# Down projections of token-tile pairs by Strassen's product in a sparse-attention and feed-forward kernel

## The chip, the core and the metric

The kernel runs on one core of a Trainium2 chip. The metric is the device time of one execution in microseconds. Five engines work side by side, each through its own in-order queue: PE (TensorE, matrix products; PEld is its weight loads), DVE (VectorE), ACT (ScalarE), POOL (GpSimd) and SP (SyncE, here a queue for transfers only). POOL's queue also issues transfers.

## The reference, cut to what matters

```python
# attention: q, k, v are [4, 8, 768, 64]; chunks of 32 keys, six chunks kept for each query
k_min, k_max = k_chunks.min(3), k_chunks.max(3)
ub = sum(max(q * k_min, q * k_max))            # a bound for each query and chunk
top_chunks = argsort(where(causal, ub, -1e9))[..., -6:]
attn = softmax(where(selected & causal, q @ k.T / 8, -1e9))
x = (attn @ v)                                 # as 3072 tokens of 512
# feed-forward: w_in is [512, 2048], w_out is [2048, 512]
h = maximum(x @ w_in, 0)
out = (h * h) @ w_out
```

The change touches the last line alone. The result is float32; inside, the kernel works in bf16 with float32 sums.

## The kernel before, in words

There are four sequences of 768 tokens, six tiles of 128 tokens each. The first tile of each sequence needs no choice of chunks (six chunks would not be exceeded); the four first tiles form a feed-forward block of their own, which runs early. Each sequence then has a block of its five other tiles. So `ffn` (L1143) is called five times.

In a block, `turn` brings a tile of x into the layout with features on partitions: through PE for the block of first tiles and for sequence 0, by a transposing transfer on SP's queue for the last three sequences. `up` (L1176) computes one of 16 slices of 128 hidden features for a group of columns (256 for the first two tiles of a sequence, 384 for the other three): four matmuls, a relu out of PSUM on ACT or DVE (L1193, L1195), and the square on DVE (L1204), which lands in a buffer of the tag `h2`. `down` (L1207) computes one token tile of the output: 16 matmuls of 128x512 that accumulate in one PSUM bank (L1217), with the squared slice as the stationary operand and a 128-row slice of `w_out` as the moving one. Then ACT or DVE copies the bank to an `ob` buffer (L387, L389), and a transfer writes it out on SP's queue, or on POOL's for sequences 1 and 2. The last tile of the kernel is done in two column groups, 384 and 128.

The attention around it: scores (L1026; for the last sequence L1083), exponentials on ACT (L1050, L1121), causal masks on POOL or DVE (L1006, L1003), products with v (L1038, L1116), normalisation on DVE (L731, L733). For the last sequence the choice of chunks goes out to a table in device memory (L967) and comes back as a mask for each head pair, by four transfers of 336 KB each on SP's queue (L974); POOL then puts the causal part into it (L1006), and DVE applies it to the exponentials (L1130).

Nothing is scheduled on the chip. Every step is recorded with `plan.op`, and the long string `SEQUENCE` lists the numbers of all steps in the order in which they are taken up, with a letter where the engine could be chosen (`A`, `D`, `G` for ACT, DVE, POOL). `Plan.order` (L220) walks through that list, gives each step a start by a table of costs, and the steps are issued sorted by these starts. So the order of each engine's queue is fixed by the list and these costs, and any change to the steps comes with a new list. Buffers have tags with a fixed number of slots, and a step that needs a slot waits until its last user is through.

```python
plan = Plan({"tp": 1, "ps": 3, "av": 2, "ff": 2, "e": 8, "h2": NFI + 6, "ht": 3,
             "ob": 3, "kq": 4, "nt": 6, "set": 3, "seen": 3,
```

`tp`, `ps`, `av` and `ff` are PSUM tags, eight banks in all. `nt` holds rows of q and k on their way to a transposing transfer.

Of the kernel before, what the change touches and what calls it, by code (L numbers as in the profile page):

```python
# [46 lines left out]
4 0 23 1 131 2 18 6 20 8 62D 7 10A 19 150 5A 22 12A 134 136 9A 135D 21 11D 13A 24 14D  # L47
3A 25 132 133D 27 61D 17D 137 16 148 26 138 146 142 147D 31 149D 143 139 174 144 29
151 145 176 140 152 141 32 177D 156 153 188 175A 154 28 157 155 178 15A 158 179 159 33
162 180 190 163D 191A 30 189D 164 184 36 192 195 193D 34 160 196A 198 161D 201 46 197  # L50
199A 194 165 202A 200 185 35 170 181 186 203 166 187 37 182 171 183 172 167 173 40 286
206 168 280 169 207A 287 41 204 290D 205A 39 288 282A 211 289D 208 45 212D 281A 213
214 209D 284 215A 217 60 226 218A 283 51 223 210 285 42 227A 219 291 224A 343 292 220
44 216 345A 293 43 229 294 344A 225 295 221A 347 296 230A 52 235 298A 346 297A 54 232
300A 228 299A 236D 38 309 317 222 310 349 237 301 48 233A 238 350 302 351 47 313 352D
318 241 348 314 353D 50 239A 305 234 322 311G 354 306 240 303G 323 355 250 67 307D 356
242A 315D 326 55 357 251A 304 308 330 324D 358 327 312 316 319 49 252 334 325 243 359
335 244 53 363D 331 362D 361D 412 332G 245A 385 336G 413 338 386 247 328G 360D 56 339
231 415D 372 248A 59 368 253 414 369 320 416D 69 373 376 249 364 406 321 374G 365 380
370G 409 256 254A 366G 65 410 367 371 375 377 389 68 262 381 408D 390 411 329 246 401  # L60
397 407D 391G 333 417 378G 398 337 255 340 469 387G 341 418 393 399G 471A 257 66 419
342 402 379 382 64 420 263 394 421 395D 388 383 422 472 392 71 396 423A 400 403 258
424D 384 435 404 427 426D 264 425D 428 473 436 448 439 449 57 470D 431 259 440 405
429G 432 474 460 437D 441D 475 260A 72 443 476 430 461 265 261 477 433G 444 70 478D
452 480 453 434 268 73 481 479A 483 462D 456 58 482 464 457 269 484 78 465 458D 438
266A 485 442 731 104 486D 267 270 487D 732A 488D 75 489D 506 450D 490 734 507 498 454G
445 271 79 499 735 491 451 98 455 494 500D 459 733D 463 495 523 492G 466 446 511 74
524 467 274 447 512 468 81 272A 737 736 525D 515 739 519 496G 502 741D 520 493 77 497
275 738 503 105 740D 513G 516 742 85 504D 527 743 501 505 528 508 521D 794 517G 509
744 83 514 518 796A 522 526 510 529 276 117 530 99 745 795A 531 277 76 746 797 80 747  # L70
534 278A 63G 749D 535A 532 748D 750D 102 533A 584 760 751D 585A 764 798 539 765 768
542 540A 799 769 800 543D 578 86 761 802 536 90 579A 544 801 752 537A 572 541 82 753
766G 580 756 538 575 573A 803D 805 804D 576A 557 108 84 757 577 545 806 558A 857 574
754G 546A 807 548 762G 858A 89 777 549D 566 808 859A 560 550 547 781 94 809 773 561A
755 860 567A 551 778 758G 103 581 774 562 779G 759 568 763 582D 782 767 785 87 775D
810 559 552A 569 279 583 812A 553 91 554 783G 811A 570D 770 861 586 555A 776 813A 815
100 563 273 771 587A 556 863 862 814D 564A 780 784 772 588 866A 789 571 638 565 589A
865 786 95 864 590 790 867D 787G 868 816 591D 106 668 819 869 669A 788 88 827 817G 870
791 593 871 670A 592 818 639 872 109 828 594D 96 820 823 671 873 596 821G 875A 101
829G 672 824 836 640 874A 825G 595 837 597D 831 674 92 792 832 598 822 605 793 678A  # L80
107 826 830 606D 840 876A 878 676 833 599 126 879 834 673 835 877A 641 607 112 677A
600D 97 882 841 1112D 886 880G 608 838D 642A 601 675 883 839 128 894 609D 602 887 1054
116 611 603A 93 1053 895 890 842G 679 124 612A 614 604 891 613 881 884G 617 1237 615A
122 127 1113A 844 620 610 888G 1236 618A 118 885 843 643 621A 899 632 619 845 892G
1055 680 623 616 633A 113 622 900 903 681 848 624A 629 119 1238 682 904 1429 907 630A
626 114 634 1114 849 852 1119A 644 846G 110 1056 683 627A 1115 645 1181A 905G 850G
1057 684 853 120 847 1240 635 685D 1174A 631 115 911 625 1060 1173A 1120D 646 123 1061
901G 1430 636A 647 1239 908 1063 637 125 688A 909G 889 1062 1243 686A 650 1244 687A
1064 912 1118 893 1065 689 1246 648A 697 651 1117 698 1245 1180A 628 851 699G 693 1247
896 854 1116 690 701 1248 855 652 856 694 691G 1175 702 705 695G 692 129 111 714 706  # L90
696 897 1121 703D 898 722 715 726 1122 700 704 121 707 716G 1123 727 902 710 906 1124
910 711 718 653 1052D 723 130 712G 1051D 719 1059D 915 656 654A 1242D 720G 649 1125
1069A 1068D 657 1234A 913D 1250D 724D 1095 916 708 1091 1066D 658 1241A 1067D 709 1126
1092 1496 1103 1249D 914 713 1251A 717 1252D 721 725 1058D 917 1096 728 1099 729 659
1104 918 1235D 730 1100 1070 919 660A 1107 1101G 662 1097D 921 1427 1071 1093G 1105G
1108 1074 1072G 1426 663 1075 920 1129A 1176 1076G 1086 1078 1127A 1082 1073 1077 972
1083 1177 664 1492 1079 1084G 665 1087 1080G 1128D 970 1428 1130A 1493 1139 666A 1131
1081 1085 1088 971 1132 1494 1431 1143 1140 1432 1094 1133G 1135 922 1433 1136 655 925
1434 923A 661 1147 1435 926A 1098 1089 928 1436 1148 1152 927 929A 1437 931 924 1153
1090 1102 1156 1141D 932A 934 930 1495 1144 937 1154D 667 933 935A 1160 1145G 938A  # L100
1106 936 940 1137G 1448 1161 943 941A 1109 1164 939 944A 1438 946 942 1110 949 1111
947A 945 1497 1178 950A 952 1498 1157 961 948 953A 1500 1158G 1134 1168 962A 1162G 954
955 1165 963 1138 1499 964 956A 1166G 1142 957 967 965A 1501 1440 951 1146 1149 1449
968A 958 1442 1155 1441 976 959A 969 1169 966 1439 960 979 1502 977A 1159 1451 973
980A 1450 978 1150 982 1452 974A 981 1179 1163 985 1470 983A 988 986A 984 975 1453
989A 991 1454 1455 994 992A 990 1167 1151 1000 995A 987 1182 996 1001A 1006 1183 993
1003 1184 1007A 1444 1170 1185 1009 1004A 1446 1002 1456 1253 1010A 1008 1012 1443
1186 1005 1015 1187 1013A 1011 1254 1265 1016D 997 1447 1457 1021 1471 1022 1017 998D
1458 1023 1190A 999 1459 1189A 1018 1266 1024 1019D 1472 1188D 1027 1191D 1025D 1503
1200 1208 1473 1028 1020 1209 1171 1014 1201 1460 1255D 1204 1172 1196 1029 1202D 1197  # L110
1205 1198G 1213 1192 1030 1206G 1193 1214 1194G 1217 1031D 1256 1278 1215G 1218 1195
1199 1203 1032 1221 1279 1462 1207 1210 1229 1222 1461 1211 1225 1219G 1212 1033 1230
1464 1223G 1267D 1226 1280G 1463 1216 1026 1257 1274 1227D 1474 1220 1224 1275 1228
1231 1269 1258 1232 1034 1233 1270 1259G 1445 1286 1282 1287 1261 1276G 1035 1262 1283
1290 1263D 1288D 1260 1264 1268 1284D 1291 1271 1277 1281 1272 1285 1289 1273 1292
1514 1293 1294 1039 1524 1295 1521 1525 1040 1518 1522 1515 1296 1041 1516 1527 1519
1347 1036 1537 1528 1469 1520 1526 1346 1037D 1531 1475 1042 1534 1538 1038 1476 1045
1345 1043A 1477 1467 1478 1044 1517 1523 1532 1297 1535 1046 1468 1298A 1529 1479 1300
1480 1540 1301A 1299 1481 1530 1302 1541 1533 1465 1303 1546 1047 1466 1304D 1554 1547
1309 1551 1555 1539 1548 1310D 1048 1552 1482 1549 1542 1306 1049A 1550 1557 1305  # L120
1307D 1553 1558 1312 1311 1308 1360 1567 1313D 1564 1559 1315 1568 1361A 1536 1543
1565 1560 1316A 1321 1561 1314 1544 1484 1318 1362 1322A 1545 1485 1570 1319A 1317
1562 1504 1556 1571 1342 1323 1486 1320 1324 1577 1343D 1483 1566 1574 1572 1563 1569
1327 1325D 1582 1573 1326 1357 1328A 1344 1575 1330 1578 1358A 1587 1329 1331A 1583
1336 1332 1597 1359 1351 1594 1337D 1591 1576 1333 1352D 1584 1579 1334A 1353 1339
1507 1585 1354 1586 1340A 1508 1338 1588 1335 1363 1505 1355A 1506 1600 1364A 1356
# [21 lines left out]
class Transfers:  # L148


    RATE = 1 / 0.00083
    SHARED = ((6.2, 0.90), (9.0, 0.95), (1e9, 1.0))
    ISSUED = {True: 0.7, False: 1.3}
    LANDED = {True: 1.3, False: 1.9}

# [156 lines left out]
def kernel(  # L312
# [943 lines left out]
    for t in range(B):  # L1256
        down(t)
# [65 lines left out]
```

## Time and profile before

| | us |
|---|---|
| runs shown: lowest, median, highest | 259.96, 260.93, 261.01 |
| profiled execution, its time | 260.51 |
| its span in the trace | 258.8 |
| granted TensorE clock, mean | 0.998 |

The 1.7 us between the profiled execution's time and its span lie outside the trace's span. A page of the profile gives the busy time of each engine, then the span in 40 slices (a digit is tenths of a slice), transfers, the chain of work that ended last, and the costliest groups of instructions. A group's row reads: line, engine, operation, output from inputs, sizes, count, busy time, mean nanoseconds of one, and the idle time just before them with what ended it. A matmul's own duration includes its way through the array, so the durations of neighbours overlap; the chain of waits shows what each adds.

### The profile page before, as it was taken

To read this page: it belongs to the slowest core of one execution; us is meant where nothing else is said; L and a number is where in the kernel's file an instruction comes from. 1 tells how busy PE (TensorE), PEld (TensorE's weight loads), DVE (VectorE), ACT (ScalarE), POOL (GpSimd) and SP (SyncE) were. 2 spreads that over 40 slices of the span, in tenths; PEclk is the share of its full clock that TensorE was granted. 3 is DMA by queue.
4 is the path that set the end of the run, shared out by engine and by line. 5 is a ranking of instruction groups with operands and counts; after the bars stand their busy time and mean duration, and the time that the engine had idled before them with its cause. 6 is when DMAs were issued, how large, how long until landed. Compare 5 with 4: busy or idle time off the path is not lost.

```text
span 258.8 us, 6699 instructions
## 1 busy us (share of the span) xinstructions
PE 248.7 (96%) x2482; PEld 159.2 (62%) x2482; DVE 202.3 (78%) x719; ACT 177.6 (69%) x352; POOL 113.6 (44%) x194
## 2 busy tenths in 40 slices
PE   8787999999999999999999999999999999999995
PEld 3555466656688666565687656656765654865543
DVE  4659999999999999999999984578978870674630
ACT  7666898598799999999997638766977630421201
POOL 8979899769855599431311304231032200010000
PEclk9999999999999999999999999999999999999999
DMA  9999999999999999994658214973993206120022
GB/s 124 128 163 162 181 171 183 180 163 160 135 177 174 159 132 128 169 123 101 85 166 182 36 25 109 206 91 117 196 188 57 85 11 153 20 81 3 7 93 103
DMA packets 117280, 31.89 MB, mean 123 GB/s; under 512 B 99840, under 2 KB 114944, under 8 KB 117248
## 3 DMA queue, kind: packets, MB, share of 16 engines
q0 software_dynamic: 77968, 16.00, 76.3%
q1 hardware_dynamic: 39280, 15.47, 31.4%
q8 instruction: 19, 0.31, 0.5%
q14 instruction: 13, 0.11, 0.2%
HBM read 32.77 MB, written 6.55 MB: 152 GB/s over the span
## 4 chain that ended last, share of the span: by engine, by line
PE 63%; DMA 14%; DVE 10%; POOL 8%; issue 2%; ACT 1%; POOLq 0%
PE py L1217 27%; PE ph L1186 20%; DMA w_in_sb<-in_moe_w_in_dram 6%; PE ps L1026 6%; PE av L1038 4%; DMA w_out_sb<-in_moe_w_out_dram 3%; DMA qt<-nt 3%; PE ps L1083 2%; DVE kr L862 2%; PE av L1116 2%; DMA nt<-in_q_dram 2%; POOL kn L574 2%; DVE kqc L389 1%; DVE h L1204 1%; POOL q L481 1%
## 5 line engine op out<-in xcount | busy, mean ns | idle before, releaser
L1186 PE MATMUL ph<-xT,w_in_sb 128*128 128x256 bf16 (+2 forms) x592 | 98.1, 304 | 1.6 <-DMA w_in_sb<-in_moe_w_in_dram 0.9
L1217 PE MATMUL py<-w_out_sb,h 128*128 128x512 bf16 (+2 forms) x400 | 93.4, 370 | 0.0
L1050 ACT ACTIVATE e<-ps 128x512 bf16<-128x512 f32 x120 | 66.4, 602 | 9.3 <-PE ps L1026 7.5
L1193 ACT ACTIVATE ht<-ph 128x256 bf16<-128x256 f32 (+2 forms) x102 | 45.1, 451 | 39.4 <-PE ph L1186 30.7
L1186 PEld LDWEIGHTS <-w_in_sb 128*128 128x128 bf16 x592 | 54.8, 97 | 26.0 <-issue 1.3
L1217 PEld LDWEIGHTS <-h 128*128 128x128 bf16 x400 | 37.0, 97 | 33.3
L1204 DVE TENSOR_TENSOR h<-ht 128x384 bf16<-128x384 bf16 (+2 forms) x148 | 46.4, 334 | 10.3 <-ACT ht L1193 9.5
L1006 POOL TENSOR_SCALAR_AFFINE_SELECT e<-e 128x128 bf16<-128x128 bf16 (+1 forms) x68 | 23.2, 352 | 44.5 <-ACT e L1050 44.1
L1026 PE MATMUL ps<-kqc 88*128 88x128 bf16 (+1 forms) x240 | 40.6, 272 | 0.0
L1195 DVE TENSOR_SCALAR ht<-ph 128x384 bf16<-128x384 f32 (+2 forms) x46 | 22.8, 497 | 15.4 <-PE ph L1186 14.6
L1038 PEld LDWEIGHTS <-e 128*128 128x128 bf16 x480 | 23.3, 97 | 6.0 <-POOL e L1006 0.2
L1026 PEld LDWEIGHTS <-kqc 88*128 88x128 bf16 x240 | 19.7, 97 | 10.7 <-DVE kqc L389 0.7
L1121 ACT ACTIVATE e<-ps 128x512 bf16<-128x512 f32 x40 | 21.2, 602 | 5.7 <-PE ps L1083 3.4
L1038 PE MATMUL av<-vn,e 128*128 128x65 bf16 x360 | 23.7, 193 | 0.1
L1006 POOL TENSOR_SCALAR_AFFINE_SELECT mask<-mask 128x256 bf16<-128x256 bf16 x20 | 9.1, 481 | 30.6 <-DMA mask<-seen 30.6
L387 ACT COPY ob<-py 128x512 f32<-128x512 f32 (+2 forms) x18 | 10.2, 564 | 14.2 <-PE py L1217 14.2
L1231 POOL DMA_DIRECT2D out_dram<-ob x10 | 5.6, 556 | 31.9 <-DVE ob L389 18.3
L733 DVE TENSOR_TENSOR x<-av,rc 128x320 bf16<-128x320 f32 (+1 forms) x40 | 18.8, 473 | 0.8
L1130 DVE TENSOR_TENSOR e<-e,mask 128x512 bf16<-128x512 bf16 x40 | 16.1, 438 | 1.6 <-ACT e L1121 1.6
L862 DVE TENSOR_REDUCE kr<-kT 128x24 bf16<-128x768 bf16 x16 | 14.7, 948 | 0.1
L567 POOL DMA_DIRECT2D vn<-in_v_dram x15 | 13.6, 911 | 0.3 <-PE av L1038 0.3
L833 DVE MAX8 m<-ubm 128x8 f32<-128x24 f32 x120 | 12.0, 168 | 0.1
(116 smaller groups left out, 319.5 us busy)
## 6 DMA issues: line engine op xcount, KB each, us to landing
mask<-seen SPq DMA_DIRECT2D x16, 336.0 KB, 6.4
out_dram<-ob SPq DMA_DIRECT2D x13, 256.0 KB, 2.3
out_dram<-ob POOLq DMA_DIRECT2D x10, 256.0 KB, 2.7
w_in_sb<-in_moe_w_in_dram POOLq DMA_DIRECT2D x4, 512.0 KB, 7.6
w_out_sb<-in_moe_w_out_dram POOLq DMA_DIRECT2D x4, 512.0 KB, 9.0
vn<-in_v_dram POOLq DMA_DIRECT2D x15, 128.0 KB, 6.6
nt<-in_q_dram POOLq DMA_DIRECT2D x10, 128.0 KB, 5.1
nt<-in_k_dram POOLq DMA_DIRECT2D x10, 128.0 KB, 6.4
```

The costliest lines, as they stand in the source:

```text
L733: return plan.op({"DVE": 0.06 + 0.00108 * D * n}, due, lambda _: nc.vector.tensor_mul(x(), av[:, :, 0:D], rc[:, 0:n].unsqueeze(2).to_broad ...
L862: nc.vector.tensor_reduce(kr[:, mm].rearrange("d (t c) -> d t c", c=128 // CH) if b >= BY_DMA else kr[:, mm], part(kT).rearrange("d t (c j ...
L1006: nc.gpsimd.affine_select(out=e, in_=e, compare_op=ALU.is_ge, fill=0.0, base=0, channel_multiplier=-1, pattern=[[0, n], [1, 128]])
L1026: nc.tensor.matmul(ps[:, 128 * c:128 * (c + nt)], lhsT=kqs(slice(0, KC), s, hh)[:, 128 * j:128 * (j + 1)], rhs=qss(slice(0, KC), s, hh)[:, ...
L1038: nc.tensor.matmul(av[:, t - 1], lhsT=e[:, 128 * c:128 * (c + 1)], rhs=value_tile(b, h, j), start=(i == 0 and c == 0), stop=(i == len(BANK ...
L1050: nc.scalar.activation(e.tile, ps.tile, ACT.Exp, scale=scale), [sc], [ps, e])
L1121: done = plan.op({"ACT": 0.487}, due + 0.5, lambda _: nc.scalar.activation(e.tile, ps.tile, ACT.Exp, scale=scale), [sc], [ps, e])
L1186: nc.tensor.matmul(ph.tile, lhsT=w_in_sb[:, ki, 128 * f:128 * (f + 1)], rhs=xT[:, c0 // 128:c1 // 128, ki], start=(ki == 0), stop=(ki == N ...
L1193: nc.scalar.activation(ht.tile, ph.tile, ACT.Relu)
L1195: nc.vector.tensor_scalar_max(ht.tile, ph.tile, 0.0)
L1204: {"DVE": 0.075 + w / 1920}, at[0] + P["h2"], lambda _: nc.vector.tensor_mul(h2[f][:, c0:c1], ht.tile, ht.tile), [op], [ht, h2[f]], port=T ...
L1217: nc.tensor.matmul(py.tile, lhsT=h2[f][:, 128 * t:128 * (t + 1)], rhs=w_out_sb[:, f, c0:c1], start=(f == 0), stop=(f == NFI - 1))
```

## The change

For the blocks of sequences 1, 2 and 3 the first four tiles are no longer done by `down` one at a time. `down_pair` takes two tiles at once and computes their 256x512 output in halves of the tokens, of the hidden features and of the output columns, by the seven products of Strassen's scheme in Winograd's form. Write A11 and A12 for the lower and upper eight hidden slices of the first tile, A21 and A22 for those of the second, and B11, B12, B21, B22 for the quarters of `w_out` (row half, column half). Then

- sums of activations: S1 = A21 + A22, S2 = S1 - A11, S3 = A11 - A21, S4 = A12 - S2;
- mixes of weights, once for all: T1 = B12 - B11, T2 = B22 - T1, T3 = B22 - B12, T4 = B21 - T2;
- products: P1 = A11 B11, P2 = A12 B21, P3 = S4 B22, P4 = A22 T4, P5 = S1 T1, P6 = S2 T2, P7 = S3 T3;
- output: C11 = P1 + P2, U2 = P1 + P6, U4 = U2 + P5, C22 = U4 + P7, U3 = U2 + P7, C21 = U3 + P4, C12 = U4 + P3.

Each product is eight matmuls of 128x256 into half a PSUM bank, in two steps of four; two products share a bank, P3 has half a bank to itself. Each sum is made in four pieces of 128x256 on DVE or POOL, as the list says; S4 overwrites S2 when P6 is through. P1 is copied into an `ob` buffer (ACT or DVE), and the output is added up there by seven additions on DVE, each with one operand in PSUM. The fifth tile is done by `down` as before.

The sums use slots of the tag `nt`, which grows from six to eight; the first tiles' transposes move from `h2` to `nt`. The squares are kept two slices to a buffer (`h2` has 10 slots of two instead of 22 of one), so that one addition can take both. The weight mixes T1, T2 and T4 are written over tensors that are no longer needed (the first tiles' x, q and k), T3 into a slot of `vn`; the built program makes them on POOL, eight subtractions of 128x1024. The planner takes other figures for early transfers and for the mask transfers, and `SEQUENCE` is rewritten throughout. In the built program 192 matmuls of 128x512 are gone and 336 of 128x256 have come; 39 pieces of sums are on DVE and 57 on POOL; nine more relus are on ACT and fewer on DVE.

```diff
@@ Transfers
     SHARED = ((6.2, 0.90), (9.0, 0.95), (1e9, 1.0))
+    EARLY = (10.0, 0.85)
...
-    plan = Plan({"tp": 1, "ps": 3, "av": 2, "ff": 2, "e": 8, "h2": NFI + 6, "ht": 3,
-                 "ob": 3, "kq": 4, "nt": 6, "set": 3, "seen": 3,
+    plan = Plan({"tp": 1, "ps": 3, "av": 2, "ff": 2, "e": 8, "h2": 10, "ht": 3,
+                 "ob": 3, "kq": 4, "nt": 8, "set": 3, "seen": 3,
...
-        t = t_first[nm, b] = buffer("h2", [128, NP, 128], name="t0")
+        t = t_first[nm, b] = buffer("nt", [128, NP, 128], name="t0")
...
-                     [w], [seen, mask], packets=1850, turns=True, free=True, late=0.2)
+                     [w], [seen, mask], packets=2250, turns=True, free=True, late=0.2)
...
-            if f not in h2:
-                h2[f] = buffer("h2", [128, 128 * n])
+            if f // 2 not in h2:
+                h2[f // 2] = buffer("h2", [128, 2, 128 * n])
+            hs = h2[f // 2]
...
+        def down_pair(t):
+            half, mid = NFI // 2, d_model // 2
+            def part_of(g, u):
+                return h2[g][:, :, 128 * u:128 * (u + 1)]
+            sums = {s: [buffer("nt", [128, 4, 128], name="s") for _ in range(2)]
+                    for s in (1, 2, 3)}
+            made_sums = {}
+            def piece(s, g):
+                return sums[s][g // 2][:, 2 * (g % 2):2 * (g % 2) + 2]
+            def add(s, g, dst, a, b, op, needs, tiles):
+                def go(e):
+                    (nc.vector if e == "DVE" else nc.gpsimd).tensor_tensor(
+                        piece(dst, g), a(), b(), op=op)
+                made_sums[s, g] = plan.op(
+                    {"DVE": 0.205, "POOL": 0.37}, at[0], go, needs, tiles, port=True)
+            quarters = half // 2
+            for g in range(quarters):
...
+                add(1, g, 1, lambda g=g: part_of(g, t + 1),
+                    lambda g=g: part_of(quarters + g, t + 1), ALU.add, two,
+                    [low, high, bufs[1]])
+                add(2, g, 2, lambda g=g: piece(1, g), lambda g=g: part_of(g, t),
+                    ALU.subtract, [made_sums[1, g]] + one, [low, bufs[1], bufs[2]])
+                add(3, g, 3, lambda g=g: part_of(g, t), lambda g=g: part_of(g, t + 1),
+                    ALU.subtract, one + two, [low, bufs[3]])
...
+            def product(bank, side, left, right, needs, tiles, before=None):
+                ops = []
+                for part in range(2):
+                    fs = range(4 * part, 4 * part + 4)
+                    def go(_, fs=fs):
+                        for f in fs:
+                            nc.tensor.matmul(
+                                bank[:, mid * side:mid * (side + 1)], lhsT=left(f),
+                                rhs=right(f), start=(f == 0), stop=(f == half - 1),
+                                skip_group_check=True)
...
+            def add_up(dst, a, bank, side, needs, tiles):
+                return plan.op(
+                    {"DVE": 0.36}, at[0] + 1, lambda _: nc.vector.tensor_tensor(
+                        dst(), a(), bank[:, mid * side:mid * (side + 1)], op=ALU.add),
+                    needs, [bank] + tiles)
...
+            p1 = product(banks[0], 0, lower(t), w(0, 0), *weights_needs(0, of_h(0, t)))
+            p2 = product(banks[0], 1, upper(t), w(1, 0), *weights_needs(1, of_h(half, t)), p1)
+            kept = plan.op({"ACT": 0.27, "DVE": 0.36}, at[0] + 1, lambda e: copy(
+                e, corner(1, 0)(), banks[0][:, 0:mid]), [p1], [banks[0], obs[1]])
+            c11 = add_up(corner(0, 0), corner(1, 0), banks[0], 1, [kept, p2], obs)
+            p6 = product(banks[1], 0, of_sum(2), mixed(2), *mixed_needs(2, of_s(2)))
...
+            p5 = product(banks[1], 1, of_sum(1), mixed(1), *mixed_needs(1, of_s(1)), p6)
+            u2 = add_up(corner(1, 0), corner(1, 0), banks[1], 0, [c11, kept, p6], [obs[1]])
+            u4 = add_up(corner(0, 1), corner(1, 0), banks[1], 1, [u2, p5], obs)
+            p7 = product(banks[2], 0, of_sum(3), mixed(3), *mixed_needs(3, of_s(3)))
+            p4 = product(banks[2], 1, upper(t + 1), mixed(4),
+                         *mixed_needs(4, of_h(half, t + 1)), p7)
...
+            p3 = product(banks[3], 0, of_sum(2), w(1, 1), *weights_needs(1, of_s(4)))
+            c12 = add_up(corner(0, 1), corner(0, 1), banks[3], 0, [c22, p3], [obs[0]])
...
+    def mix_weights():
...
+        for i, a, b, n in ((1, w(0, 1), w(0, 0), None), (2, w(1, 1), combos[1].view, 1),
+                           (3, w(1, 1), w(0, 1), None), (4, w(1, 0), combos[2].view, 2)):
+            for part in range(2):
...
+                combos[i].ops.append(plan.op(
+                    {"DVE": 0.605, "POOL": 1.06}, 0, go,
+                    free_at[i] + loaded["out", part] + loaded["out", 2 + part]
+                    + ([combos[n].ops[part]] if n else []), combos[i].tiles, port=True))
...
-        for t in range(NS - last):
+        if b in P["pairs"]:
+            if not combos:
+                mix_weights()
+            down_pair(0)
+            down_pair(2)
+        for t in range(4 if b in P["pairs"] else 0, NS - last):
             down(t)
```

## The prediction

> **What bounds the kernel now.** I read the page first: busy time, then the slices.
>
> ```profile
> span 258.8 us, 6699 instructions
> PE 248.7 (96%) x2482; PEld 159.2 (62%) x2482; DVE 202.3 (78%) x719; ACT 177.6 (69%) x352; POOL 113.6 (44%) x194
> ...
> PE   8787999999999999999999999999999999999995
> ...
> DVE  4659999999999999999999984578978870674630
> ```
>
> TensorE is full from the fifth slice to the last but one. DVE is as full up to the twenty-fourth slice, and half empty later. The view by stretches gives sizes (columns: stretch, its length, then busy time and count of PE, PEld, DVE, ACT, POOL):
>
> ```profile
> 0.00:20.00 20.00, 15.25 (x156) 8.87 (x156) 10.41 (x47) 13.43 (x22) 17.39 (x27) 1.00 1.65 137
> 20.00:40.00 20.00, 18.62 (x174) 11.60 (x175) 19.14 (x67) 16.48 (x32) 18.55 (x27) 1.00 1.73 173
> ...
> 100.00:120.00 20.00, 19.88 (x193) 11.94 (x192) 19.52 (x90) 19.27 (x38) 9.60 (x18) 1.00 1.76 145
> ...
> 140.00:160.00 20.00, 20.00 (x168) 11.97 (x167) 15.97 (x66) 11.87 (x25) 3.32 (x9) 1.00 0.31 61
> 160.00:180.00 20.00, 20.00 (x249) 12.54 (x248) 13.61 (x50) 13.66 (x27) 6.49 (x15) 1.00 0.79 153
> 180.00:200.00 20.00, 20.00 (x246) 13.62 (x240) 16.46 (x52) 15.92 (x36) 3.86 (x9) 1.00 0.82 143
> 200.00:220.00 20.00, 20.00 (x182) 10.84 (x181) 11.16 (x32) 7.44 (x14) 2.61 (x5) 1.00 0.28 81
> 220.00:240.00 20.00, 20.00 (x137) 13.16 (x135) 12.72 (x38) 5.58 (x14) 1.07 (x2) 1.00 0.12 34
> 240.00:259.00 19.00, 15.64 (x94) 8.35 (x92) 6.28 (x15) 2.60 (x6) 0.00 (x0) 0.97 0.18 69
> ```
>
> Busy time of a pipelined TensorE need not be work at full rate, so I went to the chain of waits (start, length, what), which counts each matmul by what it adds:
>
> ```profile
> 131.69 0.88 PE ph L1186 x8
> ...
> 132.91 0.87 PE ph L1186 x8
> ...
> 233.33 0.65 PE ph L1186 x4
> 233.98 1.73 PE py L1217 x8
> 235.71 0.65 PE ph L1186 x4
> 236.36 0.86 PE py L1217 x4
> ```
>
> Each piece starts where the one before ends: 233.33 + 0.65 = 233.98, + 1.73 = 235.71, + 0.65 = 236.36. Nothing stands between matmuls. So in the stage of the down projections a microsecond of TensorE work is worth a microsecond, unless another engine takes over.
>
> **What leaves and what enters TensorE.** Rows of the groups by shape (mean ns of one before the second bar):
>
> ```profile
> L1217 PE MATMUL py<-w_out_sb,h 128*128 128x512 bf16 x368 | 89.9, 379 | 0.0
> L1217 PEld LDWEIGHTS <-h 128*128 128x128 bf16 x400 | 37.0, 97 | 33.3
> L1186 PE MATMUL ph<-xT,w_in_sb 128*128 128x256 bf16 x288 | 39.1, 272 | 1.5 <-DMA w_in_sb<-in_moe_w_in_dram 0.9 <-ACT xT L387 0.4
> ```
>
> The changed program has 176 matmuls of 128x512 in place of 368: 192 leave (six pairs, two tiles, sixteen each). The chain prices them at 1.73/8 = 0.216 us, together 41.5. In come 6 x 7 x 8 = 336 of 128x256. I take their price from the pieces of eight above, which are 128x256 with a new weight each: 0.875/8 = 0.109 us, together 36.7. Difference: 4.8 us less. Bounds: at half a wide matmul (0.108) it is 5.2. If the 144 additional weight loads (97 ns by the row) were not hidden, it would be 4.8 - 14.0, a loss of 9.2; I take the first price, as the pieces of eight hold eight such loads each and still take 0.109 a matmul. The cover is thin, 97 under 109, but it is the same cover.
>
> The Trainium skill ("TensorE: Matmul & The Clock Gate", The mechanism) says that weight loads overlap running matmuls only where their row groups differ; all 128 rows are used here, so that rule would give the loss of 9.2 us. The pieces of eight contradict it.
>
> **What DVE and POOL get.** Per pair, 16 additions of 128x256 bf16 form the mixed activations (96 in all; the built order has 39 on DVE, 57 on POOL). Once, eight subtractions of 128x1024 on POOL mix the weights. Twelve evictions of 128x512 turn into six copies and 42 additions of 128x256 that read PSUM, all 42 on DVE. The nearest rows:
>
> ```profile
> L1204 DVE TENSOR_TENSOR h<-ht 128x256 bf16<-128x256 bf16 x72 | 19.1, 290 | 2.8 <-ACT ht L1193 2.4
> L887 DVE TENSOR_TENSOR ubm<-ub,ubmask 128x240 f32<-128x240 f32 x12 | 4.8, 397 | 0.9 <-PE ub L827 0.8
> L389 DVE COPY ob<-py 128x512 f32<-128x512 f32 x7 | 4.8, 690 | 6.7 <-PE py L1217 6.7
> L1195 DVE TENSOR_SCALAR ht<-ph 128x384 bf16<-128x384 f32 x24 | 13.3, 555 | 4.6 <-PE ph L1186 4.0
> L1006 POOL TENSOR_SCALAR_AFFINE_SELECT mask<-mask 128x256 bf16<-128x256 bf16 x20 | 9.1, 481 | 30.6 <-DMA mask<-seen 30.6
> L1006 POOL TENSOR_SCALAR_AFFINE_SELECT e<-e 128x128 bf16<-128x128 bf16 x55 | 18.1, 336 | 36.4 <-ACT e L1050 36.0
> ```
>
> DVE gains 42 x 0.397 = 16.7 and 39 x 0.290 = 11.3. It loses seven 128x512 evictions (4.8; three smaller ones, 1.4 as an estimate from the 128x384 row, stay) and nine relus that the new order gives to ACT (some 4.9). Net 17.9. From 140 us on its six stretches add up to 76.2; with 17.9 that is 94 of the 115 us then left, 82%. Between 100 and 120 us it ran at 19.52 of 20 while PE kept 19.88. So this lies beside PE's work and costs nothing by itself. If the cover were gone (DVE at 97%, its limit there), the surplus would go to PE.
>
> POOL: no row shows a two-input operation. Below stands 0.336 us, above 0.928 (longest mask, below); I take 0.48 for 128x256, the row of that size: 57 x 0.48 = 27 us. The step from 128x128 to 128x256 gives 1.1 ns a column, so 1.35 us for each 128x1024, 11 us together (bounds 0.3 and 3.7 each, from 0.336 at any width to four of 0.928). In the order the mixes stand before any pair product, the last of them with some 16 us of matmuls between, and POOL is idle half of 100 to 120 us (9.60 of 20). Behind each mix queue the causal masks of the scores and the loads; the nearest mask needed after one has 1.4 us of matmuls ahead of its use. I add nothing, at most 1 us.
>
> Does POOL hold up DVE? Shortest, median and longest of one, in ns:
>
> ```profile
> L1130 DVE TENSOR_TENSOR e<-e,mask x40: 381/418/649, 167.9 to 210.7; 128x512 bf16<-128x512 bf16 x40
> L1006 POOL TENSOR_SCALAR_AFFINE_SELECT mask<-mask x20: 396/412/928, 144.9 to 201.9; 128x256 bf16<-128x256 bf16 x20
> ```
>
> Equal work takes up to 0.23 us more than the median on DVE, up to 0.52 on POOL. These rows look like two engines in each other's way.
>
> **The new joints.** A product waits for its sums, and the second half of a bank often for ACT's or DVE's work. In the new order most sums stand 2 to 14 us of matmuls ahead of their product, the shortest near 1. Such a hand-over, where it does show now:
>
> ```profile
> PEld L1026 <- DVE kqc L389: 0.7, 2, 0.4
> ```
>
> That is 0.35 us. Of 42 products I let three wait so: 1.0 us. Bounds: 0, and 4 us if eleven wait.
>
> **What is only moved.** The whole issue order is rewritten, also where nothing else changes. The planner's new transfer figures reach the chip only through it.
>
> ```profile
> 16.66 1.05 PE L1186 MATMUL ph<-xT,w_in_sb 128*128 128x256 bf16 x8 [0.93 <-DMA w_in_sb<-in_moe_w_in_dram]
> ...
> 43.07 1.03 PE L1217 MATMUL py<-w_out_sb,h 128*128 128x512 bf16 x4
> ```
>
> Up to 40 us PE idles 4.75 + 1.38 = 6.1 us. The new order has the same loads, two or three fewer ahead of the first piece of w_out, and equal PE work before the first py. I take 0; a reshuffle can win or lose perhaps a quarter of that idle time, 1.5 us.
>
> The masks of the last sequence are the one late transfer chain on SP's queue. Its four loads stay in place; in the order eleven POOL operations (six before) now stand between two neighbouring PE steps there.
>
> ```profile
> 197.84 1.67 POOL L1006 TENSOR_SCALAR_AFFINE_SELECT mask<-mask 128x256 bf16<-128x256 bf16 x4 [5.05 <-DMA mask<-seen]
> ...
> 204.27 1.03 PE L1217 MATMUL py<-w_out_sb,h 128*128 128x512 bf16 x4
> ```
>
> The masks were ready at 199.5, and PE came to that step at 204.27: 4.8 us of cover. Two pairs done earlier take 1.6 of it. So 0 here, and up to 2 us if the chain slips by 5.
>
> The end: both last evictions go from ACT to DVE.
>
> ```profile
> 254.82 0.48 ACT L387 COPY ob<-py 128x384 f32<-128x384 f32 x1 [7.33 <-PE py L1217]
> 255.67 0.27 ACT L387 COPY ob<-py 128x128 f32<-128x128 f32 x1 [0.37 <-PE py L1217]
> ```
>
> The first has ended before the second may start, with 0.37 us to spare, against some 0.1 longer on DVE. Nothing added.
>
> **The sum.** The profiled execution took 260.51 us (258.8 of it span): 260.5 - 4.8 + 1.0 = 256.7. It stands 0.4 under the median 260.93, inside the spread of the runs, so I say 256.8.
>
> **The rivals.** (a) DVE becomes the bound. If each POOL sum holds it up for its whole 0.48 us, DVE has 57 x 0.48 = 27.4 us more: 121.4 against 97% of 115, 111.6, so PE waits 9.8: 260.5 - 4.8 + 9.8 = 265.5, slower. Place: the pair stretches from 150 us on. PE starts to wait at 17.6/57 = 0.31 us a sum, and the gain is gone from 0.39. For: 0.928 and 0.649. Against: those are extremes, the medians stand near the minima, and a POOL operation often meets an idle DVE or one that reads PSUM. The Trainium skill ("GPSIMD Engine Reference", Elementwise — side-by-side cycle accounting) gives 4497 ns for a two-input addition of 2048 columns; an estimate by it is 0.56 us for 256, and with whole holds the sum would be 270. No row here shows such an operation.
>
> (b) The joints eat the gain: eleven of 42 wait, 4 us: 260.5 - 4.8 + 4.0 = 259.7, no change. For: the sums are made on two in-order queues. Against: PE's short waits now, and the distances in the order.
>
> (c) Weight loads show: 260.5 + 9.2 = 269.7. Against it the pieces of eight.
>
> (d) The rewritten order also takes 1.5 us of the early idle time away: 255.2.
>
> (e) The mask chain slips: 256.7 + 2 = 258.7.
>
> (f) The change doesn't do what it says, for instance that direct products remain: excluded, 176 and 336 are in the built program.
>
> **How the numbers follow.** Forecast 0.62, (a) 0.12, (b) 0.13, (c) 0.01, (d) 0.08, (e) 0.04. A measurement of this kernel can tell 0.5%, 1.3 us, from no change: faster is below 259.6, slower above 262.2. Forecast, (d) and (e) are faster, 0.74; (b) lies at that line, a third of it goes there, and as much is taken off for cases not thought of. (a) and (c) are slower, 0.13; what is left of (b) is the same, 0.13. The range runs from 254.6 (5.2 less on PE, no joint, half the early gain) through (b) to 261.5, where holds of 0.41 us would put (a); it leaves out most of (a), (c) and the far end of (d), under 0.2. The forecast's own range is 255.3 to 258.5.
>
> **What would show it.** Right: 336 py matmuls of 128x256 in pieces of eight at 0.87 us on the chain, PE at 20.00 of 20 from 150 us on, the same 43 us before the first py, DVE near 82% after 140 us. Wrong: PE idle behind DVE's sums or POOL's (joints); DVE at 97% with 128x256 additions far over 0.29 (a); pieces of eight above 0.95 us (c); POOL's additions near 0.9 us.

## The result, and the profile after

| | before | changed |
|---|---|---|
| runs, median (lowest to highest), us | 260.97 (259.96 to 261.10) | 288.97 (288.36 to 290.20) |
| profiled execution, span, us | 258.8 | 288.5 |
| granted TensorE clock, mean | 0.998 | 0.976 |

The changed kernel takes 1.109 times as long, interval 1.1034 to 1.1146. Its figures are of three runs; a fourth, at 293.19 us, fell into a slower state and is left out of every comparison here. The forecast was 256.8, the range 254.6 to 261.5.

The page of the changed kernel, its busy time and its slices:

```profile
span 288.5 us, 7218 instructions
PE 255.6 (89%) x2641; PEld 176.3 (61%) x2641; DVE 244.2 (85%) x796; ACT 181.2 (63%) x362; POOL 168.1 (58%) x247
...
PE   7789999999998799799895988799999896998885
...
DVE  3479999799999999999999798598998994789642
PEclk9999999999999999889997799999999997999999
```

PE has gaps in many slices where it had none, and they begin near 85 us, long before the first of the new products. The view by stretches (columns as before; the last numbers are clock, DMA share, GB/s) shows how much:

```profile
80.00:100.00 20.00, 16.64 (x174) 10.87 (x172) 19.73 (x50) 14.47 (x30) 13.88 (x19) 1.00 1.35 141
100.00:120.00 20.00, 17.72 (x168) 10.44 (x166) 19.72 (x68) 16.44 (x33) 15.33 (x19) 1.00 1.26 111
...
140.00:160.00 20.00, 15.21 (x148) 10.73 (x145) 18.98 (x63) 9.74 (x25) 9.52 (x12) 0.88 0.41 96
...
220.00:240.00 20.00, 16.21 (x194) 11.69 (x193) 19.45 (x43) 8.67 (x18) 11.78 (x19) 1.00 0.07 27
```

Read the counts beside the busy times. Between 100 and 120 us DVE was busy for 19.52 us with 90 instructions; now it is busy for 19.72 with 68. It is not doing more, its instructions take longer. The groups by shape say which:

```profile
L1434 POOL TENSOR_TENSOR x<-w_out_sb 128x1024 bf16<-128x1024 bf16 x2 | 4.3, 2137 | 0.0
L1244 POOL TENSOR_TENSOR s<-h,h 128x256 bf16<-128x256 bf16 x16 | 11.2, 703 | 29.3 <-DVE h L1225 16.9 <-PE py L1280 9.4 <-PE av L1133 3.0
L1225 DVE TENSOR_TENSOR h<-ht 128x384 bf16<-128x384 bf16 x64 | 28.0, 450 | 3.8 <-ACT ht L1214 3.8
L1225 DVE TENSOR_TENSOR h<-ht 128x256 bf16<-128x256 bf16 x72 | 22.9, 341 | 1.1 <-ACT ht L1214 0.7
L886 DVE TENSOR_TENSOR kbd<-kr,own 128x96 bf16<-128x96 bf16 x12 | 5.4, 446 | 0.0
L1317 DVE TENSOR_TENSOR ob<-ob,py 128x256 f32<-128x256 f32 x42 | 17.1, 415 | 15.1 <-PE py L1280 11.3 <-DMA out_dram<-ob 2.7 <-issue 0.9
L879 DVE TENSOR_REDUCE kr<-kT 128x24 bf16<-128x768 bf16 x16 | 14.9, 949 | 0.1
```

A mix takes 2.14 us and a sum 0.70 on POOL. On DVE the square of 128x256 has gone from 290 to 341 ns on average. The additions with an operand in PSUM, at 415, are where the prediction had them (397). In the list of PE's waits for other engines the longest total is for those additions on DVE; for POOL's masks PE waits little (total, times, longest, in us):

```profile
PE py L1280 <- DVE ob L1317: 9.6, 12, 2.4
...
PE av L1055 <- POOL e L1023: 1.4, 2, 0.8
```

What an average hides is seen in the order of time (start, length, engine, what; in brackets the idle time before it and what ended it):

```profile
117.96 2.18 POOL L1434 TENSOR_TENSOR q<-w_out_sb,x 128x1024 bf16<-128x1024 bf16 x1
...
118.09 0.18 DVE L748 RECIPROCAL rc<-av 128x5 f32<-128x5 f32 x1
...
118.19 2.13 DVE L895 TENSOR_SCALAR qm<-qt 128x640 bf16<-128x640 bf16 x1
...
120.38 0.20 PE L844 MATMUL ub<-kbd,qm 128*128 128x48 bf16 x1 [1.70 <-DVE qm L895]
...
234.99 1.30 POOL L1244 TENSOR_TENSOR s<-h 128x256 bf16<-128x256 bf16 x2
...
235.10 3.83 DVE L1244 TENSOR_TENSOR s<-h 128x256 bf16<-128x256 bf16 x1
236.25 1.29 POOL L1244 TENSOR_TENSOR s<-h,h 128x256 bf16<-128x256 bf16 x2
...
237.50 0.66 POOL L1244 TENSOR_TENSOR s<-s,h 128x256 bf16<-128x256 bf16 x1
238.12 0.66 POOL L1244 TENSOR_TENSOR s<-h 128x256 bf16<-128x256 bf16 x1
...
240.18 0.38 PE L1280 MATMUL py<-q,s 128*128 128x256 bf16 x2 [2.39 <-DVE ob L1317]
```

At 117.96 POOL begins a mix that ends at 120.14. DVE's scaling of q, 0.32 us in the median, begins at 118.19 and ends at 120.32, 0.18 us after the mix. PE needs its result and idles 1.70 us. At 235.10 a sum on DVE, 0.28 us in the median, takes 3.83: six sums ran on POOL one behind another until 238.78, and DVE did not get in between them. PE idles 2.39 us. This is the extreme of the 39 sums on DVE; none of the others took more than 0.80 us. The Trainium skill ("SBUF — State Buffer", Who interferes with whom) describes this as an exclusive lock on ports that DVE and GpSimd share, held for the whole instruction. The first case agrees; in the second the wait outlasts five instruction ends, though by these rows each POOL sum begins some 0.04 us before the one ahead of it has ended.

The new products themselves are as cheap as forecast. From the chain of waits:

```profile
270.57 0.65 PE ph L1207 x4
271.22 0.47 PE py L1280 x4
271.69 0.02 issue
271.71 0.43 DVE ob L1317
272.15 0.04 issue
272.19 1.47 PE py L1280 x12
...
275.83 2.63 PE py L1280 x24
```

2.63/24 is 0.110 us a matmul. But at 271.7 PE waits for an addition on DVE, in the middle of a product, and starts again late: the twelve matmuls after it take 1.47, not 12 x 0.109 = 1.31.

### The profile page after: what moved, and what is told of

Read it like the earlier page. It is cut to its first block, busy times and chain, and to the rows that moved or that the text cites. A ratio compares the mean times of both kernels' runs of the same rounds, so it can differ in the third digit from the quotient of the medians.

```text
span 288.5 us, 7218 instructions
## 1 busy us (share of the span) xinstructions
PE 255.6 (89%) x2641; PEld 176.3 (61%) x2641; DVE 244.2 (85%) x796; ACT 181.2 (63%) x362; POOL 168.1 (58%) x247
## 5 line engine op out<-in xcount | busy, mean ns | idle before, releaser
L1207 PE MATMUL ph<-xT,w_in_sb 128*128 128x256 bf16 (+2 forms) x592 | 102.1, 309 | 9.0 <-ACT ht L1214 5.5
L1214 ACT ACTIVATE ht<-ph 128x256 bf16<-128x256 f32 (+2 forms) x111 | 49.6, 454 | 46.4 <-PE ph L1207 32.2
L1225 DVE TENSOR_TENSOR h<-ht 128x256 bf16<-128x256 bf16 (+2 forms) x148 | 55.6, 395 | 5.0 <-ACT ht L1214 4.5
L1371 PE MATMUL py<-w_out_sb,h 128*128 128x512 bf16 (+2 forms) x208 | 48.9, 367 | 0.1
L1317 DVE TENSOR_TENSOR ob<-ob,py 128x256 f32<-128x256 f32 x42 | 17.1, 415 | 15.1 <-PE py L1280 11.3
L1244 POOL TENSOR_TENSOR s<-h,h 128x256 bf16<-128x256 bf16 x16 | 11.2, 703 | 29.3 <-DVE h L1225 16.9
L1371 PEld LDWEIGHTS <-h 128*128 128x128 bf16 x208 | 18.7, 98 | 14.4 <-issue 0.9
L1280 PEld LDWEIGHTS <-s 128*128 128x128 bf16 x192 | 18.6, 100 | 12.9 <-issue 8.5
L1216 DVE TENSOR_SCALAR ht<-ph 128x256 bf16<-128x256 f32 (+2 forms) x37 | 17.8, 482 | 3.8 <-PE ph L1207 3.3
L404 ACT COPY ob<-py 128x512 f32<-128x512 f32 (+1 forms) x16 | 8.3, 519 | 15.4 <-PE py L1371 12.4
L1280 PEld LDWEIGHTS <-h 128*128 128x128 bf16 x144 | 13.6, 97 | 7.1 <-issue 4.6
L1357 POOL DMA_DIRECT2D out_dram<-ob x10 | 5.6, 558 | 20.7 <-DVE ob L1317 10.4
```

What stands on the lines that cost most here:

```text
L1207: nc.tensor.matmul(ph.tile, lhsT=w_in_sb[:, ki, 128 * f:128 * (f + 1)], rhs=xT[:, c0 // 128:c1 // 128, ki], start=(ki == 0), stop=(ki == N ...
L1214: nc.scalar.activation(ht.tile, ph.tile, ACT.Relu)
L1225: {"DVE": 0.075 + w / 1920}, at[0] + P["h2"], lambda _: nc.vector.tensor_mul(hs[:, f % 2, c0:c1], ht.tile, ht.tile), [op], [ht, hs], port= ...
L1280: nc.tensor.matmul(bank[:, mid * side:mid * (side + 1)], lhsT=left(f), rhs=right(f), start=(f == 0), stop=(f == half - 1), skip_group_chec ...
L1317: {"DVE": 0.36}, at[0] + 1, lambda _: nc.vector.tensor_tensor(dst(), a(), bank[:, mid * side:mid * (side + 1)], op=ALU.add),
L1371: nc.tensor.matmul(py.tile, lhsT=h2[f // 2][:, f % 2, 128 * t:128 * (t + 1)], rhs=w_out_sb[:, f, c0:c1], start=(f == 0), stop=(f == NFI - 1))
```

## The experiments

Three theories. H: POOL's operations hold DVE's, and PE then waits for DVE. L: POOL's results only come too late, for the plan counted 0.37 us a sum and 1.06 a mix. W: POOL has no part; additions, joints and the rewritten order cost it.

**1. Who makes the sums and mixes.** Four versions of the changed kernel with its issue order kept: in all_on_dve both edits below, in sums_on_dve the first alone, in mixes_on_dve the second alone. In no_sums neither operation is issued, and the products read other operands in their place.

```diff
@@ add
-                    (nc.vector if e == "DVE" else nc.gpsimd).tensor_tensor(
+                    nc.vector.tensor_tensor(
                         piece(dst, g), a(), b(), op=op)
@@ mix_weights
-                    (nc.vector if e == "DVE" else nc.gpsimd).tensor_tensor(
+                    nc.vector.tensor_tensor(
                         combos[i].view()[:, fs], a()[:, fs], b()[:, fs], op=ALU.subtract)
@@ no_sums: of_sum, mixed
-                return lambda f: sums[s][f // 4][:, f % 4]
+                return lambda f: ident
...
-                return lambda f: combos[i].view()[:, f]
+                return w(0, 1)
```

> The changed kernel, issue order kept, with the 57 sums and 8 mixes issued on DVE instead of POOL. Theory H (a two-input operation on POOL holds DVE's two-input operations): the 29 us by which DVE's instructions are longer than before go away, 16.5 us of sums (57 x 0.29) and 6.2 us of mixes (8 x 0.78, an estimate from the square of 128x512 at 0.418) come; DVE busy 235 to 240 us, PE full again between 80 and 120 us, time 266 to 274. Theory L (POOL's results only come too late, 0.69 us a sum and 2.15 a mix where the plan counted 0.37 and 1.06): nothing is late any more, 260 to 266. Theory W (the additions out of PSUM, the joints and the rewritten order cost it, POOL has no part): DVE has 23 us more of its own, 289 or more.

> The changed kernel, order kept, only the 8 mixes of 128x1024 issued on DVE; the 57 sums stay on POOL. H: the holds between 80 and 160 us go, some 10 us of them by the mixes, the mixes' own 6 us come; most of the 11.5 us that PE lost between 80 and 160 us comes back: 277 to 283. L: the first product that needs a mix comes long after it, and PE waits for POOL's causal masks only 1.4 us in all: 286 to 289. W: 289 to 292.

> The changed kernel, order kept, only the 57 sums issued on DVE; the 8 mixes stay on POOL. H: the loss between 80 and 140 us stays (PE 16.6 and 17.7 of 20 in the stretches 80 to 100 and 100 to 120); later 16 us of holds go and 16.5 us of sums come, DVE stays about as full, 280 to 288. L: the sums are no longer late, PE's waits for DVE's additions go: 270 to 277. W: 289 to 295.

> The changed kernel with the 96 sums and 8 mixes left out: products with a sum read the constant identity in its place, products with a mix read a quarter of w_out; the order of all else, the 42 additions out of PSUM and every matmul are kept. H and L: 256 to 259, what the prediction's sum gave for PE and the joints. W: 270 or more.

| version | median, us | against the changed kernel | ratio to before |
|---|---|---|---|
| all_on_dve | 271.86 | -17.1 | 1.0435 (1.0387 to 1.0482) |
| mixes_on_dve | 280.07 | -8.9 | 1.0731 (1.0670 to 1.0793) |
| sums_on_dve | 281.03 | -7.9 | 1.0768 (1.0706 to 1.0831) |
| no_sums | 263.89 | -25.1 | 1.0130 (1.0070 to 1.0191) |

The three moves to DVE fall in H's intervals, and nearly add up: 8.9 + 7.9 = 16.8 against 17.1. L and W are outside in all three: the mixes matter by 8.9 us, although PE's own waits for POOL's masks came to 1.4. In all_on_dve DVE was given 65 more instructions, and by the page it is less busy than the 244.2 us above:

```profile
PE 249.4 (92%) x2625; PEld 175.1 (65%) x2641; DVE 232.3 (86%) x861; ACT 181.3 (67%) x362; POOL 110.5 (41%) x182
```

Alone, a mix takes DVE 0.68 us and a sum 0.29 (that run's groups):

```profile
L1434 DVE TENSOR_TENSOR mix<-w_out_sb 128x1024 bf16<-128x1024 bf16 x2 | 1.4, 683 | 0.0
L1244 DVE TENSOR_TENSOR s<-h,h 128x256 bf16<-128x256 bf16 x24 | 6.9, 293 | 0.1
```

No theory had no_sums right: it stays 7 us above the forecast with neither sums nor mixes. Its list of PE's waits (total, times, longest) names most of the reason:

```profile
PE py L1279 <- DVE ob L1316: 4.5, 8, 1.1
...
PE py L1279 <- ACT ob L404: 0.7, 2, 0.5
```

**2. The hold without anybody waiting for a result.** The kernel before, with operations added on POOL whose result nothing reads, at the planned times of the mixes (88.9 to 138.3 us) or sums (137 to 246). They write over the first tiles' x, which is no longer needed there. The list `todo` holds the planned times; a dummy sum is a dummy mix of 128x256, the 57 memsets are 128x512.

```diff
@@ write
+            while todo and todo[0] <= op.start:
+                todo.pop(0)
+                self.extra()
             for t in op.tiles:
@@ extra, before_8_dummy_mixes
+        nc.gpsimd.tensor_tensor(scratch[:, 0:4], w_out_sb[:, 0:4, 0:256],
+                                w_out_sb[:, 0:4, 256:512], op=ALU.subtract)
@@ extra, before_8_memsets
+        nc.gpsimd.memset(scratch[:, 0:8], 0.0)
@@ extra, before_8_selects
+        nc.gpsimd.affine_select(
+            out=x_first[:, 0:4], in_=x_first[:, 0:4], compare_op=ALU.is_ge, fill=0.0,
+            base=0, channel_multiplier=1, pattern=[[0, 4], [0, 512]])
```

> The kernel before, with eight subtractions of 128x1024 bf16 added on POOL at the planned times of the mixes (88.9 to 138.3 us); nothing reads their result. H: each lasts 2.1 to 2.2 us and holds DVE's two-input operations; DVE's excess grows by 8 to 12 us in the stretches where it is full, time 267 to 273. L: only the causal masks queued behind them come late, 261 to 264. W: 261.

> The kernel before, with eight memsets of 128x2048 bf16 on POOL in the same places: POOL is busy about as long (an estimate of 2.2 us each from the memset of 128x128, 0.27 us, less a start of 0.1) but reads nothing. H: DVE is not held, its rows are as before, 261 to 263. L: the same delay of what is queued behind on POOL as with the subtractions, so the same time as that run. W: 261.

> The kernel before, with 57 subtractions of 128x256 bf16 added on POOL at the planned times of the sums (137 to 246 us); nothing reads their result. H: DVE's excess grows by 57 x 0.28 = 16 us or less, but DVE has 35 us of room after 140 us in this kernel, so the time moves by 0 to 6 us: 261 to 267. L: 261 to 263, only the masks of the last sequence are queued behind. W: 261.

> The kernel before, with 57 memsets of 128x512 bf16 on POOL in the places of the sums, about as long (an estimate of 0.6 us) but reading nothing. H: DVE's rows stay as before, 261 to 262. L: as with the subtractions. W: 261.

> The kernel before, with eight affine selects of 128x2048 bf16 in place on POOL where the dummy mixes stood: one input from SBUF instead of two, about as long or longer (2.5 us each, an estimate from 0.336 at 128 columns and 0.481 at 256). If every POOL operation that reads SBUF holds DVE's two-input operations for its whole length: 273 to 277, DVE's excess 12 us and more over before. If only two-input operations do: 263 to 265, as with the memsets.

| added on POOL | each, us | median, us | over before (260.57; selects 260.52) | DVE busy (202.3 before) |
|---|---|---|---|---|
| 8 dummy mixes | 2.16 | 273.51 | 12.9 | 214.3 |
| 8 memsets | 1.82 | 263.09 | 2.5 | 205.1 |
| 8 selects, one input | 1.95 | 270.96 | 10.4 | 213.1 |
| 57 dummy sums | 0.69 | 267.95 | 7.4 | 213.0 |
| 57 memsets | 0.53 | 261.62 | 1.1 | 202.1 |

DVE has the same 719 instructions in each of these. Eight subtractions that nobody waits for make them 12.0 us longer and the kernel 12.9 us slower; memsets that keep POOL's queue busy about 85% as long cost 2.5 (76% and 1.1 for the 57). So what is queued behind POOL explains little, and the hold most: 12.9 - 2.5 + 7.4 - 1.1 = 16.7 us. The 17.1 that came back when POOL was relieved are near it, but are not the same quantity: DVE's own time for the 65 operations is already taken off them. The dummy mixes and sums lie 0.5 and 1.0 us above H's intervals, the 8 memsets 0.1; L had wanted memsets and subtractions equal. The selects fall between the two forecasts, nearer to the one that every reading operation holds.

Two rows of DVE, by shape, first with dummy mixes:

```profile
L873 DVE TENSOR_REDUCE kr<-kT 128x24 bf16<-128x768 bf16 x16 | 14.8, 949 | 0.1
L880 DVE TENSOR_TENSOR kbd<-kr,own 128x96 bf16<-128x96 bf16 x12 | 5.5, 455 | 0.1
```

with memsets (and the copy that grew most there, from 352 ns before to 664):

```profile
L872 DVE TENSOR_REDUCE kr<-kT 128x24 bf16<-128x768 bf16 x16 | 14.8, 949 | 0.1
L879 DVE TENSOR_TENSOR kbd<-kr,own 128x96 bf16<-128x96 bf16 x12 | 3.0, 247 | 0.1
L393 DVE COPY kqc<-kt 64x768 bf16<-64x768 bf16 x4 | 2.7, 664 | 0.1
```

and with selects:

```profile
L881 DVE TENSOR_TENSOR kbd<-kr,own 128x96 bf16<-128x96 bf16 x12 | 5.2, 436 | 0.1
```

A product of two SBUF operands goes from 247 ns beside memsets to 455 beside subtractions and to 436 beside selects. The reduction, with one operand, stays at 949. So the hold falls on DVE instructions with two SBUF operands (and on some copies and scalings), and it comes from POOL instructions that read SBUF with one input as well as with two. Memsets are not wholly free either: with them two shapes of copies and one of scalings make up 2.3 of the 2.8 us that DVE gains. The same section of the Trainium skill states both: a DVE instruction with two SBUF inputs contends with a GpSimd instruction that reads SBUF, not with one that only writes it; and the trace agrees, 247 against 455.

**3. The joints.** In the order as built, the read of a bank's first half is issued between the two steps of the product in its second half. Dependences are kept by bank, so the second step waits for the read. Here the reads are issued behind that product, and whatever needs them follows (`plan.now` is the planned start of the step being issued):

```diff
@@ Plan
+    def emit(self, op):
+        last = next((n for n in [getattr(op, 'after', None)] + op.needs
+                     if n is not None and n not in self.out), None)
+        if last is not None:
+            self.held.setdefault(last, []).append(op)
+            return
+        op.fn(op.engine)
+        self.out.add(op)
+        for other in self.held.pop(op, ()):
+            self.emit(other)
@@ down_pair
+            kept.after, u2.after, c22.after, u3.after = p2, p5, p4, p4
@@ relu, dve_joined_relu alone
-                if e == "ACT":
+                if e == "ACT" or plan.now > 140.0:
```

> no_sums again (sums and mixes left out, identity and a quarter of w_out read in their place), with one thing changed: the read of a bank's first half (the copy of P1, U2, C22, U3) is issued after the last matmul of the product in its second half, not between that product's two steps. If the joints are that place (theory J: the second step waits until DVE or ACT has read the other half of its bank, 0.4 to 0.5 us each time, 5.2 us in all in no_sums), 3 to 5 us go: 259 to 261. If the waits are for a free bank at the start of a product (theory B), nothing changes or the later reads make it worse: 263.5 to 266.

> all_on_dve with the same move of the reads behind the second product. If the joints and DVE's load add up: 271.9 less what no_sums_joined gains, 267 to 269. If DVE's lateness covers the joints: 270.5 to 272.

> dve_joined with every relu planned after 140 us on ACT, which is 40% busy there, 0.45 us instead of 0.55 on DVE. If what is left over no_sums is DVE's load after 140 us, some 8 us of DVE work less give back half of that: 263 to 266. If it is the mixes and sums standing ahead of DVE's other work before 140 us, no change: 267 to 269.

no_sums_joined took 262.87: one microsecond less than no_sums, between the two theories. The reads no longer stand in the middle of products, but other waits came or stayed, because the reads are now later on DVE:

```profile
PE ph L1219 <- DVE ht L1228: 1.7, 3, 1.0
PE py L1291 <- DVE ob L1328: 1.6, 3, 1.0
...
PE ph L1219 <- DVE ob L1328: 0.8, 1, 0.8
```

With the sums on DVE the move is worth more: dve_joined took 267.45, 4.4 under all_on_dve. That lies in the first interval, but not for its reason: 271.9 less the 1.0 that no_sums_joined gains would be 270.9. Why the move gains four times as much here was not tested. dve_joined_relu, 267.79, is no better, although DVE's busy time fell from 231.7 to 223.4. So DVE's load after 160 us is not what still costs. (Between 140 and 160 us DVE stayed full, 19.80 of 20 us before the relus moved and 19.64 after.) Between 80 and 160 us PE is busy 75.4 us of 80 in dve_joined and 78.8 in no_sums_joined, which points to the mixes and first sums in the stretch where DVE is full. This part was not isolated.

No version measured beats the kernel before. The fastest that makes all sums and mixes, dve_joined, has a ratio of 1.0276 (1.0250 to 1.0302). One with fewer pairs was not tried; each pair can save 0.8 us on PE, and no_sums_joined, with nothing to add on DVE or POOL, is still 2.3 us slower than before.

## Why the prediction was wrong

**Right.** PE's price: 0.110 us a matmul, so 4.7 us of PE work leave, and the weight loads stay hidden; rival (c) falls. The additions out of PSUM: 0.415 us against 0.397. The early part: up to 40 us PE idles 5.7 us in the changed kernel, 6.1 before; rival (d) falls. The mask chain: no mask of the last sequence is in the list of PE's waits; rival (e) falls.

**The step that failed** is "Does POOL hold up DVE?". The sum has no term for it, and it stood only as rival (a), with a chance of 0.12. It costs 17.1 us of the 32.2 between forecast and result, by taking POOL's sums and mixes away; adding such operations to the kernel before costs 16.7, net of the memsets. The prediction saw it in its two rows ("two engines in each other's way") and set it aside, because "those are extremes, the medians stand near the minima". These medians say only that a mask of 0.41 us on POOL seldom meets a two-input instruction on DVE. The change put operations of 0.70 and 2.14 us on POOL, and the rows above show DVE waiting nearly as long as they run (2.13 us beside a mix of 2.18).

The plan has the hold mostly on the wrong engine. In `Plan.order`, a step marked `port` on DVE that overlaps one on POOL makes the one on POOL longer, never itself. On the chip the eight mixes on POOL all took 2.12 to 2.18 us, while DVE beside them was stretched. So the new issue order left DVE no time for the hold.

Rival (a) came near the size of the hold, 27.4 us, but by luck. From the pages: no_sums has DVE at 209.5; 104 sums and mixes bring it to 232.3, 0.22 each on average, so the 39 sums that the changed kernel has on DVE make some 8.6 (an estimate, as a mix is longer than a sum), and 244.2 - 209.5 - 8.6 = 26.1 is left for the hold. But (a) counted sums alone. In the kernel before, 57 sums made DVE 10.7 us longer, and the eight mixes, for which (a) had nothing, 12.0.

Its time of 265.5 failed for two reasons. It left out the mixes, which cost 8.9 us alone: their planned times lie in stretches where DVE had less than one microsecond of room in 20. And it let a hold cost only what exceeds 97% of DVE's time, while PE waits for one certain instruction: the 57 dummy sums cost 7.4 us beside a DVE with some 35 us of room after 140 us.

**Prices of POOL's work**: 0.70 us a sum and 2.14 a mix, against 0.48 and 1.35, inside the bounds. By itself this is the small part: memsets in the same places, 76 and 85% as long, cost 1.1 and 2.5 us.

**DVE has room.** The 82% after 140 us was taken as cover. (The net gain behind it adds up to 18.3 us, not 17.9; nothing hangs on this.) With all sums and mixes on DVE, where POOL's cannot hold it, all_on_dve is still 8.0 us above no_sums. The average over 115 us hid this: in all_on_dve DVE is busy for 19.60 of the 20 us from 140 to 160. In dve_joined it is 19.80, and taking 8.3 us of relus off DVE, nearly all of it later, gained nothing. Which of DVE's instructions PE pays for stays open.

**The joints** were mis-sized, 1.0 us, bounds 0 to 4. no_sums shows ten waits of 5.2 us in all, and each costs some 0.16 more until PE is in step again (1.47 against 1.31): 6.8 us where the forecast had 1.0. That is 5.8 of the 7.1 us by which no_sums misses it; the other 1.3 were not traced. The prediction named both places, the sums and the shared banks, but let only three of 42 products wait, 0.35 us each; the waits sit at the banks shared by two products. In one of the ten, 1.10 us, the addition itself had waited for a transfer out of its `ob` buffer. The 6.8 us are what the waits add up to, not what a cure gave: issuing the reads later returned 1.0 in no_sums. The Trainium skill ("PSUM — Partial Sum Buffer", PSUM bank collisions raise a hardware error) asks for a guard by bank, whatever columns are touched. The waits here are of that kind; what happens without them was not tried.

So the 32.2 us are 7.1 that are there without any sum, most of it joints by PE's waits, 8.0 for the sums and mixes as DVE work, and 17.1 for having most of it on POOL.

## What to carry to other kernels

Work moved to POOL is not free work beside DVE: price each POOL operation that reads SBUF with up to its whole length on DVE, and look in which stretch DVE has that time to give. Measured here in DVE's busy time: 12.0 us for 17.3 of mixes beside a full DVE, 10.7 for 39.5 of sums beside one with room. When a profile's longest durations stand far over the median on both of two engines, ask what length of operation would make the exception the rule. Where dependences are kept by bank, two products in one PSUM bank tie the second product's matmuls to the first one's reader.

## What the runs showed of the hardware

Two things were not expected. The first is the hold over several instructions, 3.83 us for an operation of 0.28, above. The second is the clock. Around some stops of PE the granted clock falls (stretches of the changed kernel, the column behind POOL is the clock):

```profile
118.00:121.00 3.00, 1.30 (x28) 1.05 (x28) 3.00 (x5) 1.12 (x3) 3.00 (x2) 1.00 0.88 129
121.00:124.00 3.00, 3.00 (x26) 1.87 (x23) 2.79 (x14) 2.11 (x4) 1.22 (x3) 0.50 0.83 72
...
238.00:240.00 2.00, 0.00 (x0) 0.00 (x0) 2.00 (x5) 0.00 (x0) 0.78 (x2) 1.00 0.00 0
240.00:242.00 2.00, 1.82 (x10) 1.32 (x10) 0.33 (x2) 0.00 (x0) 0.79 (x2) 0.62 0.33 66
```

After the stop of 1.70 us shown above come three microseconds at half clock. The same happens around stops of 2.60 us (ending at 156.78) and 2.39. But after one of 1.88 us that ends at 97.35 the clock stays at 1.00, so the length of one stop does not decide it, and what does was not worked out. The Trainium skill ("TensorE: Matmul & The Clock Gate", Part 1: The HAM clock gate) gives an idle window of about 3.4 us before the half clock; here one half as long was enough in the first case.

Over the kernel PE is busy 255.6 us against 249.4 in all_on_dve, which issues the same matmuls at a clock of 1.0. How much of these 6 us the kernel's time felt is open: three runs of the changed kernel at a mean clock of 0.976, 0.981 and 0.993 took 290.20, 288.36 and 288.97 us.
